# Spreading the rows of max plus log-sum over SBUF: from eight partitions instead of from DRAM

## The chip, the cores and the metric

The kernel runs on one core of one Trainium2 chip. A core has TensorE (PE; PEld is its weight load), VectorE (DVE), ScalarE (ACT), GpSimd (POOL), SyncE (SP, which issues every DMA of this kernel) and 16 DMA engines. The metric is the device time of one execution in microseconds; lower is better.

## The reference

For 8 batches, 8 heads, 576 tokens and a head width of 64, a linear attention is followed by a gated mixing layer:

```python
q_s = exp(q - max(q, -1)); q_s = q_s / (sum(q_s, -1) + 1e-09)      # over a head's 64 channels
k_s = exp(k - max(k, 2));  k_s = k_s / (sum(k_s, 2) + 1e-09)       # over the 576 tokens
kv  = einsum('bhsd,bhse->bhde', k_s, v)
x   = einsum('bhsd,bhde->bhse', q_s, kv)        # heads laid side by side: (B, S, 512)
gate = sigmoid(causal 5-tap convolution of x along the tokens, a tap per channel)
out  = (gate * (x @ w_val)) @ w_out             # all float32
```

## The kernel before

Everything works by batch and, inside a batch, by four blocks of 128 channels (two heads each); a block holds all 576 tokens in the free dimension. Each engine runs its instructions in the order in which a hand-written list, `ORDER`, names the steps (`name batch block engine`); nothing is reordered afterwards. An engine that waits holds up all that stands behind it on that engine. Matmuls take float32 split into a high and a low part (`x_high`, `x_low` and so on), so every product is three matmuls.

The softmax of q runs along the channels of a head, but the attention matmul (`attend`) wants channels on partitions. For batches 4 to 7 the kernel therefore computes, with tokens on partitions, the max (`q_max`), the exponentials and their sum (`q_total`), takes the logarithm (`q_log`, on ACT), and brings max plus log of the sum to the channel layout, where `l_sub` subtracts it from q as loaded by channel (`load_qc`) and `c_exp` takes the exponential: exp(q - max - log sum) is the softmax. The steps that bring it there are the ones changed:

- `l_turn` (L403): one addition of `qm` and `qs` into the tile `lse` (128 tokens by head and chunk of 128 tokens), and four 32 by 64 transposes on DVE into `lt`, a buffer of the rotating two-buffer tag `far`. Then a row of `lt` holds 128 tokens of one head.
- `l_row` (L411): two DMAs write those 40 rows into a DRAM tile `lrow`, a head's five chunks one behind the other.
- `l_spread` (L418): DMAs read a head's row from DRAM once for each of the 64 partitions of the head and so fill `lb` (128 partitions, four blocks, 576 tokens; 1.18 MB). The even heads go to partitions 0 to 63 and the odd heads to 64 to 127. The last 64 tokens of an odd batch sit in the row of the even batch before it, so an even batch takes two DMAs and an odd batch four.
- `l_sub` (L428): four subtractions `qc - lb` per batch, one per channel block, on POOL or DVE.

The tag `far` is also used by the convolution: `far` (ACT, L574) writes one scaled tap into a buffer of it, and `near` (POOL, L579) adds that to the gate. With two buffers, the second `far` after an `l_turn` gets the buffer in which `lt` was.

All DMAs go out on SP in list order, on one hardware queue, and the program has eight DMA semaphores that the DMAs take in turn: one DMA is not issued before the one eight places ahead of it has landed.

Of the kernel before, what the change touches and what calls it, by code (L numbers as in the profile page):

```python
# [7 lines left out]
F32 = mybir.dt.float32  # L8
# [8 lines left out]
B, H, S, D = 8, 8, 576, 64  # L17
C = H * D
P = 128
NB = C // P  # L20
MAIN = 4 * P
# [5 lines left out]
PITCH = 5 * P  # L27
# [123 lines left out]
def gated_linear_attention(ctx: ExitStack, tc: tile.TileContext, q, k, v, qt, kt, vt, qc, kc, km, w_val, w_out, ident_in, out):  # L151
    nc = tc.nc

    const = ctx.enter_context(tc.tile_pool(name="const", bufs=1))
# [3 lines left out]
    rowpool = ctx.enter_context(tc.tile_pool(name="rowpool", bufs=1, space=bass.MemoryType.DRAM))  # L158
# [5 lines left out]
    def block(tag, name, bufs, dtype=F32, n=S):  # L164
        return work.tile([P, S], dtype, tag=tag, name=name, bufs=bufs)[:, :n]
# [21 lines left out]
    T = {}  # L187
# [7 lines left out]
    def q_parts(b):  # L195
        return 5 if b % 2 == 0 else 4
# [204 lines left out]
    def l_turn(b):  # L401

        n = q_parts(b)  # L403
        lse, turned = lses[b % 2], T.setdefault(("lt", b), block("far", f"lt_{b}", 2)[:32, :2 * P].rearrange("p (k r) -> p k r", k=2))
        by_chunk = [t[:, :n * H].rearrange("p (c h) -> p c h", h=H) for t in (T["qm", b], T["qs", b])]
        nc.vector.tensor_add(lse[:, :5 * H].rearrange("p (h c) -> p c h", c=5)[:, :n], *by_chunk)
        for g in range(4):
            gs = slice(32 * g, 32 * g + 32)
            nc.vector.transpose(turned[:, :, gs], lse[gs].rearrange("p (k r) -> p k r", k=2))

    def l_row(b):  # L411

        t = T["lrow", b] = rowpool.tile([H * PITCH], F32, tag=f"lrow{b}", name=f"lrow{b}")
        rows_of = t.rearrange("(r s) -> r s", s=P)
        nc.sync.dma_start(out=rows_of[:32], in_=T["lt", b][:, 0])
        nc.sync.dma_start(out=rows_of[32:], in_=T["lt", b][:5 * H - 32, 1])

    def l_spread(b):  # L418
        t = big.tile([P, 5, C], F32, tag="q", name=f"lb{b}").rearrange("p c j -> p (c j)")[:, :NB * S]
        t = T["lb", b] = t.rearrange("p (n s) -> p n s", n=NB)  # L420
        pieces = [(b, 0, slice(0, S))] if b % 2 == 0 else [(b, 0, slice(0, MAIN)), (b - 1, S, slice(MAIN, S))]
        for j in range(2):
            for row, at, cs in pieces:
                n = cs.stop - cs.start
                one = T["lrow", row].rearrange("(p j s) -> j p s", j=2, s=PITCH)[j:j + 1, :, at:at + n]
                nc.sync.dma_start(out=t[D * j:D * j + D, :, cs], in_=one.broadcast_to([D, NB, n]))

    def l_sub(b, p, e="p"):  # L428
        t = T["qc", b, p]
# [214 lines left out]
        [const.tile([P, NB, C], F32R, tag=f"{w}_{x}", name=f"{w}_{x}") for x in ("hi", "lo")]  # L644
        for w in ("w_val", "w_out")
    ]
    lses = [const.tile([P, 64], F32, tag=f"lse{i}", name=f"lse{i}") for i in range(2)]
    kvd = [const.tile([P, NB, P], F32, tag=f"kvd{i}", name=f"kvd{i}") for i in range(2)]
    ktz = [const.tile([P, C], F32, tag=f"ktz{i}", name=f"ktz{i}") for i in range(2)]
    nc.scalar.preload_act_table(AF.Exp)  # L650
    for t in kvd + ktz + lses:
        nc.gpsimd.memset(t, 0.0)

    with tc.manual_schedule():
# [51 lines left out]
```

## Time and profile before

| | us |
|---|---|
| median of the runs (308.83 to 309.14) | 308.99 |
| profiled execution | 311.52 |
| its span | 309.6 |
| PE busy | 275.5 (89%) |
| DVE busy | 270.4 (87%) |
| ACT busy | 223.6 (72%) |
| POOL busy | 220.4 (71%) |
| mean rate of the DMAs | 196 GB/s |

The span is the time from the first to the last instruction of the profiled execution; 1.9 us of its time lie around it. A row of a timeline gives the start, the duration, the engine, the source line, and, in brackets, how long the engine was idle ahead of it and what ended that. In a row of windows, the last three numbers are the granted TensorE clock, the busy share of the 16 DMA engines and the rate that they moved.

### The profile page before, as it was taken

Reading aid. Unit: us, or ns where it says so; the run is one execution under the profiler, and the core shown is the slowest. Engines: PE = TensorE matmul, PEld = TensorE weight load, DVE = VectorE, ACT = ScalarE, POOL = GpSimd, SP = SyncE. Lnnn points to the kernel's source line nnn. Section 1 sums busy time; section 2 is a strip of 40 time slices with the busy share of each in tenths; the row PEclk is TensorE's granted clock in tenths of the full one; section 3 lists DMA queues with packets and bytes.
Section 4 is the critical chain, followed back from the end, with each engine's and each line's share of the span. In section 5 each row is a group of like instructions: output and inputs, shape, how many; then the busy total and the mean of one; then the engine's idle time right before and its main releaser. Section 6 shows DMA issues by size and latency. Waiting matters only on the chain.

```text
span 309.6 us, 6401 instructions
## 1 busy us (share of the span) xinstructions
PE 275.5 (89%) x2464; PEld 266.5 (86%) x2464; DVE 270.4 (87%) x371; ACT 223.6 (72%) x356; POOL 220.4 (71%) x196
## 2 busy tenths in 40 slices
PE   0176899999999999799977999997989999999995
PEld 0066699999999999799966999897989999999994
DVE  3899999999999997999899999999998898777721
ACT  2898999949997798779966697894966694426100
POOL 4678777799987998894989439596469856925600
PEclk9997999999999999889999799999999999999999
DMA  7999622688829999537867786895159330011012
GB/s 213 407 412 372 229 92 70 282 249 310 293 26 376 286 389 296 236 98 177 274 257 173 152 266 216 290 228 217 16 181 238 100 116 2 8 71 76 2 45 108
DMA packets 23278, 60.77 MB, mean 196 GB/s; under 512 B 4272, under 2 KB 4816, under 8 KB 20560
## 3 DMA queue, kind: packets, MB, share of 16 engines
q1 hardware_dynamic: 23248, 60.37, 60.0%
q8 instruction: 19, 0.31, 0.4%
q14 instruction: 11, 0.09, 0.1%
HBM read 50.83 MB, written 9.53 MB: 195 GB/s over the span
## 4 chain that ended last, share of the span: by engine, by line
PE 62%; DVE 18%; DMA 9%; ACT 4%; issue 4%; POOL 1%; SPq 1%; DVEq 0%; ACTq 0%
PE out L595 26%; PE val L595 24%; PE kv L468 5%; PE x L548 5%; DVE gate L572 3%; DMA k<-in_k 3%; DMA kc<-in_k_channels 3%; DMA q<-in_q 3%; PE qTps L500 2%; DVE g L613 2%; DMA out<-o 2%; DVE gl L621 1%; DVE q L375 1%; DVE x L567 1%; DVE qm L370 1%
## 5 line engine op out<-in xcount | busy, mean ns | idle before, releaser
L595 PE MATMUL val<-x,w_val_hi 128*128 128x288 f32 x512 | 88.4, 294 | 0.0
L572 DVE SCALAR_TENSOR_TENSOR gate<-x,cw,gate 128x574 f32<-128x574 f32 (+3 forms) x103 | 82.4, 808 | 2.4 <-ACT far L577 0.7
L595 PEld LDWEIGHTS val<-x,w_val_hi 128*128 128x128 f32 x512 | 74.8, 188 | 0.0
L595 PE MATMUL out<-gh,w_out_lo 128*128 128x288 f32 x256 | 57.4, 304 | 2.6 <-DVE g L613 1.9
L595 PE MATMUL val<-x,w_val_lo 128*128 128x288 f32 x256 | 55.4, 297 | 3.0 <-DVE o L177 1.8
L595 PE MATMUL out<-gh,w_out_hi 128*128 128x288 f32 x256 | 56.1, 299 | 0.0
L595 PEld LDWEIGHTS out<-gh,w_out_lo 128*128 128x128 f32 x256 | 41.8, 191 | 4.4 <-issue 2.1
L581 POOL TENSOR_TENSOR gate<-gate,far 128x572 f32<-128x572 f32 (+3 forms) x25 | 34.2, 1371 | 15.9 <-ACT far L577 10.7
L595 PEld LDWEIGHTS val<-x,w_val_lo 128*128 128x128 f32 x256 | 40.8, 188 | 3.8 <-ACT gate L584 1.9
L595 PE MATMUL out<-gl,w_out_hi 128*128 128x288 f32 x256 | 41.1, 302 | 1.9 <-DVE gl L621 1.9
L595 PEld LDWEIGHTS out<-gh,w_out_hi 128*128 128x128 f32 x256 | 42.2, 192 | 0.0
L595 PEld LDWEIGHTS out<-gl,w_out_hi 128*128 128x128 f32 x256 | 37.4, 196 | 2.3 <-DVE gl L621 2.3
L621 POOL TENSOR_TENSOR gl<-g,gh 128x576 fp32r<-128x576 f32 x19 | 27.6, 1459 | 12.4 <-ACT gh L175 7.0
L175 ACT COPY o<-out 128x576 f32<-128x576 f32 (+1 forms) x24 | 15.1, 629 | 26.8 <-PE out L595 16.6
L375 POOL TENSOR_TENSOR q<-q,qm 128x512 f32<-128x512 f32 x28 | 31.3, 1130 | 3.8 <-PE val L595 2.3
L310 POOL TENSOR_TENSOR k<-k,kmax 128x512 f32<-128x512 f32 x21 | 28.3, 1359 | 2.7 <-DMA kmax<-krow 2.6
L613 DVE TENSOR_TENSOR g<-val,gate 128x576 f32<-128x576 f32 x32 | 23.8, 749 | 7.0 <-PE val L595 6.8
L584 ACT ACTIVATE gate<-gate 128x576 f32<-128x576 f32 x32 | 21.5, 682 | 10.7 <-DVE gate L572 6.9
L577 ACT ACTIVATE far<-x,cw 128x572 f32<-128x572 f32 (+3 forms) x25 | 18.6, 743 | 13.4 <-DVE gate L563 4.8
L430 POOL TENSOR_TENSOR qc<-qc,lb 128x576 f32<-128x576 f32 x13 | 18.9, 1464 | 10.1 <-DMA qc<-in_q_channels 9.1
L370 DVE TENSOR_REDUCE qm<-q 128x8 f32<-128x512 f32 (+3 forms) x12 | 20.8, 1743 | 4.9 <-DMA q<-in_q 3.2
L567 DVE TENSOR_TENSOR x<-x,x 128x576 fp32r<-128x576 f32 x32 | 23.9, 748 | 0.1
(108 smaller groups left out, 556.5 us busy)
## 6 DMA issues: line engine op xcount, KB each, us to landing
out<-o SPq DMA_DIRECT2D x31, 288.0 KB, 3.9
v<-in_v SPq DMA_DIRECT2D x8, 1040.0 KB, 7.5
q<-in_q SPq DMA_DIRECT2D x7, 1024.0 KB, 7.6
km<-in_k_strided SPq DMA_DIRECT2D x24, 288.0 KB, 5.7
k<-in_k SPq DMA_DIRECT2D x6, 1024.0 KB, 7.8
qc<-in_q_channels SPq DMA_DIRECT2D x16, 288.0 KB, 4.9
kc<-in_k_channels SPq DMA_DIRECT2D x8, 288.0 KB, 8.1
lb<-lrow SPq DMA_DIRECT2D x4, 576.0 KB, 7.5
```

The costliest lines, as they stand in the source:

```text
L310: engine(e).tensor_sub(kk[r, cs], kk[r, cs], mx[r, cs])
L370: nc.vector.tensor_reduce(out=T["qm", b][:, cs], in_=qq, axis=AX.X, op=ALU.max, negate=b < 2)
L375: engine(e).tensor_tensor(qq, qq, m, op=ALU.add if b < 2 else ALU.subtract)
L430: engine(e).tensor_sub(t, t, T["lb", b][:, p])
L567: nc.vector.tensor_sub(xl, T["x", b, p], T["xh", b, p].bitcast(F32))
L572: nc.vector.scalar_tensor_tensor(out=a, in0=x, scalar=w, in1=a, op0=ALU.mult, op1=ALU.add)
L577: nc.scalar.activation(T["far", b, p, j], T["x", b, p][:, :S - n], AF.Copy, scale=cw[:, p, j:j + 1])
L581: nc.gpsimd.tensor_add(a, a, T["far", b, p, j])
L584: nc.scalar.activation(T["gate", b, p], T["gate", b, p], AF.Sigmoid)
L595: nc.tensor.matmul(ps[:, cs], a[:, kb, ms], z[:, cs], start=(i == 0), stop=(i == len(parts) - 1))
L613: nc.vector.tensor_mul(T["g", b, m], T["val", b, m], T["gate", b, m])
L621: engine(e).tensor_sub(T["gl", b, m], T["g", b, m], T["gh", b, m].bitcast(F32))
```

## The change

`l_turn` now transposes into partitions 32 to 63 of the whole `far` buffer. Its rows are ordered by head and chunk with four chunks a head; the fifth chunk, which only even batches have, is added by an instruction of its own and lies in eight further rows. There is one `lse` tile where there were two.

`l_row` no longer writes to DRAM. One DMA gathers, inside the same buffer, the four pieces of each head into one row on partitions 0 to 7, a partition for each head. In an even batch a second DMA brings the first half of the fifth chunk behind it, and a third saves the second half, the tail of the odd batch, in a small tile `ltail`; an odd batch fetches its tail from `ltail`.

`l_spread` issues eight DMAs, one for each head, in the order of the heads. Each reads one partition's row of 576 numbers 64 times and writes it to the 64 partitions of the head: 144 KB each.

```diff
     def l_turn(b):
 
         n = q_parts(b)
-        lse, turned = lses[b % 2], T.setdefault(("lt", b), block("far", f"lt_{b}", 2)[:32, :2 * P].rearrange("p (k r) -> p k r", k=2))
-        by_chunk = [t[:, :n * H].rearrange("p (c h) -> p c h", h=H) for t in (T["qm", b], T["qs", b])]
-        nc.vector.tensor_add(lse[:, :5 * H].rearrange("p (h c) -> p c h", c=5)[:, :n], *by_chunk)
+        t = T["lt", b] = block("far", f"lt_{b}", 2)
+        qm, qs = (x[:, :4 * H].rearrange("p (c h) -> p c h", h=H) for x in (T["qm", b], T["qs", b]))
+        nc.vector.tensor_add(lse[:, :32].rearrange("p (h c) -> p c h", c=4), qm, qs)
+        if n == 5:
+            nc.vector.tensor_add(lse[:, 32:32 + H], T["qm", b][:, 4 * H:], T["qs", b][:, 4 * H:])
+        k = n - 3
         for g in range(4):
             gs = slice(32 * g, 32 * g + 32)
-            nc.vector.transpose(turned[:, :, gs], lse[gs].rearrange("p (k r) -> p k r", k=2))
+            out = t[32:64, :k * P].rearrange("p (k r) -> p k r", k=k)[:, :, gs]
+            nc.vector.transpose(out, lse[gs, :32 * k].rearrange("p (k r) -> p k r", k=k))
 
     def l_row(b):
 
-        t = T["lrow", b] = rowpool.tile([H * PITCH], F32, tag=f"lrow{b}", name=f"lrow{b}")
-        rows_of = t.rearrange("(r s) -> r s", s=P)
-        nc.sync.dma_start(out=rows_of[:32], in_=T["lt", b][:, 0])
-        nc.sync.dma_start(out=rows_of[32:], in_=T["lt", b][:5 * H - 32, 1])
+        t = T["lt", b]
+        nc.sync.dma_start(out=t[:H, :MAIN], in_=t[32:64, :P])
+        if b % 2 == 0:
+            nc.sync.dma_start(out=t[:H, MAIN:], in_=t[32:32 + H, P:P + 64])
+            nc.sync.dma_start(out=ltail, in_=t[32:32 + H, P + 64:2 * P])
+        else:
+            nc.sync.dma_start(out=t[:H, MAIN:], in_=ltail)
 
     def l_spread(b):
         t = big.tile([P, 5, C], F32, tag="q", name=f"lb{b}").rearrange("p c j -> p (c j)")[:, :NB * S]
         t = T["lb", b] = t.rearrange("p (n s) -> p n s", n=NB)
-        pieces = [(b, 0, slice(0, S))] if b % 2 == 0 else [(b, 0, slice(0, MAIN)), (b - 1, S, slice(MAIN, S))]
-        for j in range(2):
-            for row, at, cs in pieces:
-                n = cs.stop - cs.start
-                one = T["lrow", row].rearrange("(p j s) -> j p s", j=2, s=PITCH)[j:j + 1, :, at:at + n]
-                nc.sync.dma_start(out=t[D * j:D * j + D, :, cs], in_=one.broadcast_to([D, NB, n]))
+        for h in range(H):
+            one = T["lt", b][h:h + 1].unsqueeze(1).broadcast_to([1, D, S])
+            nc.sync.dma_start(out=t[D * (h % 2):D * (h % 2) + D, h // 2], in_=one)
...
-    lses = [const.tile([P, 64], F32, tag=f"lse{i}", name=f"lse{i}") for i in range(2)]
+    lse = const.tile([P, 64], F32, tag="lse", name="lse")
+    ltail = const.tile([H, 64], F32, tag="ltail", name="ltail")
...
-    for t in kvd + ktz + lses:
+    for t in kvd + ktz + [lse]:
```

On SP, around the spread of batch 4 (`lt_4` is the transposed tile, `lb4` the spread one, `kmax_5` the spread max of k, `out_0` the result), there stood before:

```order
L300 DMA krow5_1755<-kpk_5_1493 128x4
L415 DMA lrow4_1765<-lt_4_1757 32x128
L416 DMA lrow4_1765<-lt_4_1757 8x128
L220 DMA qc_4_0_1811<-in_q_channels 128x576
L638 DMA out_0<-o_2_1_1780 128x576
L426 DMA lb4_1823<-lrow4_1765 64x4x576 x2
L220 DMA qc_4_2_1896<-in_q_channels 128x576
L213 DMA q6_1898<-in_q 128x2048
```

And now:

```order
L300 DMA krow5_1754<-kpk_5_1492 128x4
L418 DMA lt_4_1756<-lt_4_1756 8x4x128
L420 DMA lt_4_1756<-lt_4_1756 8x64
L421 DMA ltail_79<-lt_4_1756 8x64
L220 DMA qc_4_0_1811<-in_q_channels 128x576
L642 DMA out_0<-o_2_1_1780 128x576
L430 DMA lb4_1823<-lt_4_1756 64x1x576 x8
L220 DMA qc_4_2_1902<-in_q_channels 128x576
L213 DMA q6_1904<-in_q 128x2048
```

No step changed its place; two DMAs have become three for the rows, and two have become eight for the spread, all ahead of the same loads. The four heads' worth of one DMA before are now four DMAs.

On DVE, the additions and transposes of batches 4 and 5 before:

```order
L406 TENSOR_TENSOR lse0_78<-qm_4_1376,qs_4_1683 128x5x8
L409 STREAM_TRANSPOSE lt_4_1757<-lse0_78 32x2x32 x4
...
L406 TENSOR_TENSOR lse1_79<-qm_5_1619,qs_5_1863 128x4x8
L409 STREAM_TRANSPOSE lt_5_1946<-lse1_79 32x2x32 x4
```

And now:

```order
L406 TENSOR_TENSOR lse_78<-qm_4_1375,qs_4_1682 128x4x8
L408 TENSOR_TENSOR lse_78<-qm_4_1375,qs_4_1682 128x8
L413 STREAM_TRANSPOSE lt_4_1756<-lse_78 32x2x32 x4
...
L406 TENSOR_TENSOR lse_78<-qm_5_1618,qs_5_1869 128x4x8
L413 STREAM_TRANSPOSE lt_5_1952<-lse_78 32x32 x4
```

An even batch has one addition more, and an odd batch transposes half as much. The orders on PE and ACT are the same as before, and so is POOL's but for one memset less. Because the spread now reads from the `far` buffer, the ACT instruction that writes that buffer next (`far 3 1 0` for batch 4) now waits for all eight spread DMAs, where before the buffer was free once the two row DMAs had landed.

## The prediction

> **What bounds the kernel now.** I read the page first, then the chain of waits, then the changed tile `lb` by itself, and last the windows and timelines around its four transfers.
>
> ```profile
> span 309.6 us, 6401 instructions
> PE 62%; DVE 18%; DMA 9%; ACT 4%; issue 4%; POOL 1%; SPq 1%; DVEq 0%; ACTq 0%
> GB/s 213 407 412 372 229 92 70 282 249 310 293 26 376 286 389 296 236 98 177 274 257 173 152 266 216 290 228 217 16 181 238 100 116 2 8 71 76 2 45 108
> ```
>
> The chain of waits runs mostly over PE, then DVE. The DMA engines reach 412 GB/s at most, so each of the 16 moves at most 412 / 16 = 25.8 GB/s. From the chain, in order of time, two pieces say which engine carries it behind the changed steps:
>
> ```profile
> 221.23 2.21 DVE qs L394
> ...
> 230.32 3.44 PE val L595 x24
> ...
> 252.25 2.48 PE kv L468 x80
> ```
>
> From 199 to 230 us the chain is DVE, from there to the end PE, and it passes through no spread. The tile `lb` by itself (instructions, then its waits, then the time from issue to landing):
>
> ```profile
> L430 POOL TENSOR_TENSOR qc<-qc,lb x13: 1404/1425/1947, 148.1 to 249.1; 128x576 f32<-128x576 f32 x13
> L426 SPq DMA_DIRECT2D lb<-lrow x12: 586/609/1162, 138.0 to 235.3; - x12
> ...
>   DMA lb<-lrow: 0.9, 1
> ...
> DMA to landing us min/median/max: 6.3/7.4/8.5
> ```
>
> Only one subtraction waits for `lb`, 0.9 us. So there is almost nothing to win by a faster spread, and a slower one is late soon. The SyncE timeline gives the issue of the four spreads, batches 4 to 7:
>
> ```profile
> 138.04 1.35 SPq L426 DMA_DIRECT2D lb<-lrow  x2
> 163.69 2.56 SPq L426 DMA_DIRECT2D lb<-lrow  x4
> 199.99 1.25 SPq L426 DMA_DIRECT2D lb<-lrow  x2
> 232.73 3.14 SPq L426 DMA_DIRECT2D lb<-lrow  x4
> ```
>
> How fast do they move? Windows, first of a stretch with 128-partition loads, then three with the spreads of batches 6 and 7 (last three numbers: clock, DMA share, GB/s):
>
> ```profile
> 196.00:200.00 4.00, 3.38 (x26) 3.14 (x24) 4.00 (x6) 3.47 (x6) 1.42 (x2) 1.00 0.99 350
> ...
> 204.00:206.00 2.00, 2.00 (x17) 2.00 (x16) 2.00 (x3) 1.71 (x4) 2.00 (x2) 1.00 1.06 222
> ...
> 236.00:238.00 2.00, 2.00 (x18) 2.00 (x17) 1.93 (x4) 1.20 (x1) 1.92 (x3) 1.00 1.05 212
> 238.00:240.00 2.00, 2.00 (x17) 2.00 (x17) 1.97 (x4) 0.00 (x0) 1.92 (x2) 1.00 1.07 211
> ```
>
> This is the row on which the forecast rests. The engines are equally busy, but a transfer that has 64 partitions at its SBUF end moves 211 to 222 GB/s, half of the 412 of the page. The rate follows the number of partitions that a DMA reaches, not the engines. The changed spread has 64 partitions at one end and **one** at the other.
>
> **The rows (`l_turn`, `l_row`).** An even batch has one addition more, an odd batch half the transposing.
>
> ```profile
> L409 DVE STREAM_TRANSPOSE lt<-lse x16: 232/233/238, 134.2 to 229.2; 32x64 f32<-32x64 f32 x16
> L406 DVE TENSOR_TENSOR lse<-qm,qs x4: 293/615/1245, 133.8 to 227.2; 128x40 f32<-128x40 f32 x2, 128x32 f32<-128x32 f32 x2
> L415 SPq DMA_DIRECT2D lrow<-lt x4: 325/359/380, 135.2 to 229.4; - x4
> SPq L426 <- DMA lrow<-lt: 3.5, 1, 3.5
> ```
>
> Two additions at 0.3 us and up to eight times 0.12 us saved cancel within 1 us. The gather costs SP a third DMA in even batches, 0.4 us by the row of L415. What could be won is the wait of SP for the rows in DRAM, 3.5 us once (the last row above), but the spread that it holds back is not waited for there. I take the steps at nothing; if the gather were as slow as DRAM, that is what the kernel has now.
>
> **The spread.** The bytes stay: 128 partitions x 4 x 576 x 4 = 1.18 MB, 147,456 B for a head. Call X the time from the issue of the first of the eight DMAs to the landing of the last. Bounds for the rate:
> - From above, the source sets no limit: 215 GB/s as in the windows, X about 1.18 MB / 215 + landing = 7 to 8.5 us, as now.
> - From below, strict proportion to the partitions: 412 / 128 = 3.2 GB/s, 46 us for one head.
> - Between them: one partition hangs on one of sixteen ways, and a way carries a sixteenth of the peak, 25.8 GB/s. Then a head takes 147,456 / 25.8e3 = 5.7 us.
>
> I take the middle one. Half the partitions gave half the rate, so the ways are limited, and the best that the trace shows one engine to carry is 25.8. The eight heads go one after the other, since all DMAs are on one queue and all engines have the first head's rows ahead of the next one's: 8 x 5.7 = 45.8, and with 1.5 us to land (144 KB stores land in 1.8 us, of which 0.4 is their bytes) X = 47.3 us.
>
> ```profile
> out<-o SPq DMA_DIRECT2D x2, 144.0 KB, 1.8
> ```
>
> [...]
>
> **What the late spread costs, batch by batch.** Rows of before, the first instructions that need the spread and what hangs on them:
>
> ```profile
> 144.54 0.78 ACT L577 ACTIVATE far<-x,cw 128x572 f32<-128x572 f32 x1
> 146.63 0.23 ACT L399 ACTIVATE qs<-qs 128x32 f32<-128x32 f32 x1
> ...
> 147.25 0.93 DVE L406 TENSOR_TENSOR lse<-qm,qs 128x32 f32<-128x32 f32 x1
> 155.29 2.82 DVE L370 TENSOR_REDUCE qm<-q 128x40 f32<-128x2560 f32 x1 [1.67 <-DMA q<-in_q_tail]
> ...
> 175.02 1.43 POOL L430 TENSOR_TENSOR qc<-qc,lb 128x576 f32<-128x576 f32 x1 [3.92 <-DMA qc<-in_q_channels]
> 176.40 1.04 POOL L375 TENSOR_TENSOR q<-q,qm 128x512 f32<-128x512 f32 x1
> 181.69 2.34 ACT L379 ACTIVATE q<-q 128x2560 f32<-128x2560 f32 x1
> 184.06 2.82 DVE L394 TENSOR_REDUCE qs<-q 128x40 f32<-128x2560 f32 x1
> ...
> 209.39 2.81 POOL L430 TENSOR_TENSOR qc<-qc,lb 128x576 f32<-128x576 f32 x2
> 212.15 1.49 POOL L375 TENSOR_TENSOR q<-q,qm 128x512 f32<-128x512 f32 x1
> 219.01 1.92 ACT L379 ACTIVATE q<-q 128x2048 f32<-128x2048 f32 x1
> ...
> 243.22 1.43 POOL L430 TENSOR_TENSOR qc<-qc,lb 128x576 f32<-128x576 f32 x1 [0.85 <-DMA lb<-lrow]
> 244.60 1.41 POOL L581 TENSOR_TENSOR gate<-gate,far 128x572 f32<-128x572 f32 x1
> 245.97 1.76 POOL L310 TENSOR_TENSOR k<-k,kmax 128x512 f32<-128x512 f32 x1
> ```
>
> - Batch 4: the `far` buffer now stays taken until the last head has landed. `far 3 1 0` on ACT (144.54, 6.5 us behind the issue) waits for it, and behind it stand the logarithm of batch 5 (146.63) and so DVE's addition (147.25). The 1.67 us for which DVE waits at 155.29 go into that. Delay X - 6.5 - 1.7 = X - 8.2.
> - Batch 5: `l_sub 5 3` on POOL needs heads 6 and 7 and the `qc` loads queued behind them, 2 x 295 KB / 350 GB/s = 1.7 us more. Then 1.4 (`l_sub`) and 1.0 (`q_sub`), and ACT can start the exponential of q, which DVE takes up at once (184.06): X + 4.1 against 181.69 - 163.69 = 18.0. Delay X - 13.9.
> - Batch 6: the two `l_sub` on POOL need `qc` loads that now land behind all heads, 0.8 us; then 2.8 and 1.5, and ACT's exponential, at 219.01 or 19.0 behind the issue, feeds DVE's sum at 221.23, in the chain. Delay X + 5.1 - 19.0 = X - 13.9.
> - Batch 7: POOL's `l_sub 7 3`, then `near` and `k_sub`, 1.4 + 1.4 + 1.8, then ACT's exponential of k, 1.9; TensorE's `kv 7` in the chain at 252.25, 19.5 behind the issue, needs it. Delay X + 6.5 - 19.5 = X - 13.0.
>
> TensorE has work queued for a few microseconds at each of these places, but DVE or PE, in the chain, stands behind each of the four. Nor can the loads behind the spread (q and k of the next batches) pass it: they land during the same stall. The sum is 4X - 49.0 = 4 x 47.3 - 49.0 = 140 us on the profiled execution's 311.5, so 452; the median of the runs is 2.5 us lower, so **449 us**. After such gaps the clock is halved for a while:
>
> ```profile
> 172.00:174.00 2.00, 2.00 (x10) 2.00 (x10) 1.96 (x4) 0.27 (x1) 0.00 (x0) 0.50 0.59 190
> ```
>
> That may cost some 2 us a gap; it is left to the range.
>
> **The rivals.**
> - *The source sets no limit*, because repeated reads of one row are served as easily as those of DRAM, or are read once. This is the other side: no slower. For it: `lb<-lrow`, too, reads each row 64 times and fills its 64 partitions at half the peak. Against it: the halving itself. Price: X is 8, every delay in the list is nil or negative, and the eight issues (8 x 0.6 = 4.9 us on SP) lie beside the transfer. What can be won is the 0.9 us at 243 us, what can be lost is 1.5 us at `far 3 1 0`. Time 308 to 313, from X under some 10 us on.
> [...]
> - *Strict proportion* or worse than a sixteenth: one partition gives less than a way does. Half a way would be 4 x 93 - 49 = 323 us more, time over 600. Nothing in the trace asks for it.
>
> **How the numbers follow.** One way, one after the other: 0.58; no limit: 0.22 (of that 0.04 faster, 0.17 the same, 0.01 slower by over 2%); two ways: 0.14; worse: 0.06. The forecast's own range is 432 (5.3 us a head, and 3 us of slack found in each batch) to 462 (2 us a gap for the clock, and some for the loads behind). To leave out no more than 2 in 10 the range goes from 310, which takes in most of the case without a limit, to 462. It is wide because the cost of reading one partition 64 times stands in no row. Within 2% is what a measurement here can't tell from no change; slower by more than that 0.58 + 0.14 + 0.06 + 0.01 = 0.79, the same 0.17, faster 0.04.
>
> **What would show it.** In the changed profile, the eight `lb<-lt` DMAs should land 5 to 6 us apart, and the windows from their issue should show the DMA rate near 26 GB/s with the engines' share near 1. ACT should wait at `far` (now L581) for `lb` or `lt` some 40 us in batch 4, POOL at `l_sub` (now L434) for `lb` over 30 us in batches 5 to 7, and PE should have four gaps. `lb` issues that land in 8 us or less, with no new wait at L434 above 2 us, would prove it wrong; landing 2.9 us apart on the mean would be the two ways.

## The result: 445 us, 1.44 times the time before

The changed kernel takes 444.88 us (443.67 to 446.08) against 308.99 us; the ratio is 1.440, with a 95% interval from 1.423 to 1.457. The forecast was 449 us. Its profiled execution took 443.67 us with a span of 441.9, so 132.3 us more than the span before.

The page of the changed kernel: the span, the rate of the DMAs in 40 slices of 11 us, and the chain of waits.

```profile
span 441.9 us, 6438 instructions
...
GB/s 270 411 306 222 93 217 326 212 248 298 360 217 92 27 37 29 198 181 49 28 32 44 261 255 120 29 33 41 191 105 127 27 34 40 116 9 55 53 2 107
...
SPq 34%; PE 27%; DMA 17%; DVE 9%; POOL 6%; issue 4%; ACT 3%; DVEq 0%; POOLq 0%; ACTq 0%
```

Before, 62% of the chain was PE and 1% SP's queue. Now 34% is SP's queue, PE is 27%. Four times the rate falls to 27 to 49 GB/s for three or four slices: those are the four spreads. Their issues in SyncE's timeline, batches 4 to 7:

```profile
138.47 31.10 SPq L430 DMA_DIRECT2D lb<-lt  x8
...
200.18 30.51 SPq L430 DMA_DIRECT2D lb<-lt  x8
...
267.30 30.55 SPq L430 DMA_DIRECT2D lb<-lt  x8
...
334.32 30.75 SPq L430 DMA_DIRECT2D lb<-lt  x8
```

The issues before were at 138.04, 163.69, 199.99 and 232.73. So the delay grows by 36.1 us behind batch 4, 30.8 behind batch 5, 34.3 behind batch 6, and from 101.6 to the 132.3 at the end, 30.7 behind batch 7. The four stalls are the whole difference. Inside the first of them, from the chain, the single issues:

```profile
138.47 0.57 SPq L430
139.09 0.58 SPq L430
139.73 1.14 SPq L430
140.91 7.92 SPq L430
148.87 5.45 SPq L430
154.37 5.44 SPq L430
159.85 4.23 SPq L430
164.12 5.44 SPq L430
```

From the fourth on, SP is held at every issue: 7.92 us at the fourth, 4.23 at the seventh and 5.44 or 5.45 at the others, instead of 0.6. 5.44 us is the pace of a head: 147,456 B in 5.44 us are 27.1 GB/s. The windows inside the stall and behind it say the same (clock, DMA share, GB/s at the end):

```profile
150.00:160.00 10.00, 0.00 (x0) 0.00 (x0) 0.00 (x0) 0.00 (x0) 0.00 (x0) 0.52 0.88 29
...
182.00:186.00 4.00, 2.92 (x54) 2.92 (x56) 3.68 (x8) 3.94 (x6) 2.89 (x3) 0.50 0.92 321
```

The 16 engines count as 88% busy and move 29 GB/s, while every compute engine stands. Who waits first, from the timelines of ACT, POOL and DVE:

```profile
181.38 0.74 ACT L581 ACTIVATE far<-x,cw 128x572 f32<-128x572 f32 x1 [37.35 <-DMA qc<-in_q_channels]
...
244.66 0.74 ACT L581 ACTIVATE far<-x,cw 128x572 f32<-128x572 f32 x1 [30.20 <-DMA qc<-in_q_channels]
...
246.26 1.40 POOL L434 TENSOR_TENSOR qc<-qc,lb 128x576 f32<-128x576 f32 x1 [39.30 <-DMA qc<-in_q_channels]
...
311.34 2.75 POOL L434 TENSOR_TENSOR qc<-qc,lb 128x576 f32<-128x576 f32 x2 [33.38 <-DMA qc<-in_q_channels]
...
312.90 0.76 DVE L177 COPY o<-out 128x576 f32<-128x576 f32 x1 [30.73 <-DMA out<-o]
...
377.96 1.40 POOL L434 TENSOR_TENSOR qc<-qc,lb 128x576 f32<-128x576 f32 x1 [35.81 <-DMA lb<-lt]
...
378.74 0.76 DVE L177 COPY o<-out 128x576 f32<-128x576 f32 x1 [32.77 <-DMA out<-o]
```

In batch 4 it is `far 3 1 0` on ACT, whose buffer the spread still reads (it waits for the eight spread DMAs; the profile names a transfer that came last with them). In batches 5, 6 and 7 it is the first `l_sub` on POOL. Beside it stand waiters that the forecast did not have. In batch 5 `far` on ACT waits 30.20 us and goes on 1.6 us before POOL does. In 6 and 7 it is DVE's copy of a result, whose buffer is free only when an earlier store has left, and that store is queued behind the spread. From first issue to the end of the wait, X is 181.38 - 138.47 = 42.9 us in batch 4 and 377.96 - 334.32 = 43.6 us in batch 7.

### The profile page after: what moved, and what is told of

It reads as the page before. It is cut to its first block, busy times and chain, and to the rows that moved or that the text cites. A ratio compares the mean times of both kernels' runs of the same rounds, so it can differ in the third digit from the quotient of the medians.

```text
span 441.9 us, 6438 instructions
## 1 busy us (share of the span) xinstructions
PE 281.5 (64%) x2464; PEld 270.9 (61%) x2464; DVE 273.5 (62%) x373; ACT 223.8 (51%) x356; POOL 221.3 (50%) x195
## 4 chain that ended last, share of the span: by engine, by line
SPq 34%; PE 27%; DMA 17%; DVE 9%; POOL 6%; issue 4%; ACT 3%; DVEq 0%; POOLq 0%; ACTq 0%
SPq L430 27%; PE val L599 12%; PE out L599 9%; DMA out<-o 7%; SPq L220 5%; DMA qc<-in_q_channels 5%; PE kv L472 2%; DMA v<-in_v 2%; DMA kc<-in_k_channels 2%; PE x L552 2%; PE qTps L504 2%; DMA q<-in_q 2%; DVE qm L370 1%; POOL k L310 1%; POOL gl L625 1%
## 5 line engine op out<-in xcount | busy, mean ns | idle before, releaser
L599 PE MATMUL val<-x,w_val_hi 128*128 128x288 f32 x512 | 91.9, 302 | 28.3 <-DVE x L571 28.3
L576 DVE SCALAR_TENSOR_TENSOR gate<-x,cw,gate 128x574 f32<-128x574 f32 (+3 forms) x103 | 82.3, 807 | 39.1 <-ACT far L581 37.4
L599 PE MATMUL val<-x,w_val_lo 128*128 128x288 f32 x256 | 58.4, 311 | 64.7 <-DVE o L177 62.0
L599 PEld LDWEIGHTS val<-x,w_val_hi 128*128 128x128 f32 x512 | 78.2, 195 | 28.5 <-DVE x L571 28.5
L599 PEld LDWEIGHTS val<-x,w_val_lo 128*128 128x128 f32 x256 | 43.2, 199 | 66.1 <-ACT qc L438 31.4
L177 DVE COPY o<-out 128x576 f32<-128x576 f32 (+1 forms) x9 | 6.5, 722 | 74.0 <-DMA out<-o 63.5
L472 PE MATMUL kv<-v,k 128*64 128x65 f32 x512 | 21.4, 235 | 38.5 <-DVE gate L576 36.7
L472 PEld LDWEIGHTS kv<-v,k 128*64 128x64 f32 x512 | 19.5, 149 | 40.3 <-DVE gate L576 36.9
L599 PE MATMUL out<-gl,w_out_hi 128*128 128x288 f32 x256 | 39.7, 295 | 1.5 <-DVE gl L625 1.5
L599 PEld LDWEIGHTS out<-gl,w_out_hi 128*128 128x128 f32 x256 | 35.7, 188 | 1.9 <-DVE gl L625 1.9
L625 POOL TENSOR_TENSOR gl<-g,gh 128x576 fp32r<-128x576 f32 x19 | 27.6, 1460 | 9.9 <-ACT gh L175 6.9
L438 ACT ACTIVATE qc<-qc 128x576 f32<-128x576 f32 x16 | 10.6, 680 | 37.2 <-POOL qc L434 37.2
```

The lines of the kernel that those rows point to most:

```text
L472: nc.tensor.matmul(acc[h * D:(h + 1) * D, p, :], T["k", b][:, c, cs] if c < 4 else ktz[b % 2][:, cs], T["v", b][:, c, hd] if c < 4 else T[ ...
L576: nc.vector.scalar_tensor_tensor(out=a, in0=x, scalar=w, in1=a, op0=ALU.mult, op1=ALU.add)
L599: nc.tensor.matmul(ps[:, cs], a[:, kb, ms], z[:, cs], start=(i == 0), stop=(i == len(parts) - 1))
L625: engine(e).tensor_sub(T["gl", b, m], T["g", b, m], T["gh", b, m].bitcast(F32))
```

## Experiments

The theory: a source partition's way into the DMA sets the pace, and all that is queued behind the spread waits with it. The rivals: the eight DMAs themselves; SBUF as a source; the single partition, or the receiving side, rather than a way that partitions share; and the waits for `lb` and for the `far` buffer rather than the queue. Where no ratio is given, the time is that of a single execution.

### The rows in DRAM again, eight DMAs kept

```diff
...
-        pieces = [(b, 0, slice(0, S))] if b % 2 == 0 else ...
...
+        row = T["lrow", b].rearrange("(h s) -> h s", s=PITCH)
+        for h in range(H):
+            one = row[h:h + 1, :S].unsqueeze(1).broadcast_to([1, D, S])
+            nc.sync.dma_start(out=t[D * (h % 2):D * (h % 2) + D, h // 2], in_=one)
```

> The kernel before, with its rows in DRAM, but with the spread issued as eight DMAs of 144 KB, one for each head, as in the changed kernel; an odd batch fetches its 64-token tail by one small DMA from DRAM to DRAM. My theory (one SBUF partition as the source of 64 reads sets the pace, 5.4 us a head): the source is DRAM again, so a spread lands in some 8 us at about 215 GB/s and the time is 308 to 314 us. The rival (eight small DMAs, their issue on SP and the eight semaphores are what costs): SP stands at each of them for about 5 us as in the changed kernel, and the time stays above 400 us.

Measured: 310.11 us, ratio 1.002 (0.998 to 1.006). The tile `lb` of this kernel:

```profile
L429 SPq DMA_DIRECT2D lb<-lrow x32: 445/594/606, 137.1 to 239.8; - x32
...
DMA to landing us min/median/max: 3.0/3.6/5.2
```

The same eight transfers, with the same 64 reads of one row, take 0.6 us to issue and land in 3.6 us when the row is in DRAM. So neither the number of DMAs nor the repeated reading as such shows in the time. The source is left.

### SBUF as the source, but 64 partitions of it

```diff
-            one = T["lt", b][h:h + 1].unsqueeze(1).broadcast_to([1, D, S])
+            one = W[0][0].bitcast(F32).rearrange("p n c -> p (n c)")[D * (h % 2):D * (h % 2) + D, :S]
```

> The changed kernel, but each of the eight DMAs of a spread reads 64 different SBUF partitions of a constant (the high part of w_val) instead of one partition 64 times; bytes, targets and number of DMAs stay. The spread rows are then not the max plus log-sum, so the output is another. My theory: 64 source partitions feed it about as fast as it is written, a spread lands in 8 us, 306 to 314 us. The rival (SBUF as a source is slow, or SBUF to SBUF at all): 440 us or near it.

Measured: 309.37 us, ratio 1.003 (0.998 to 1.008). The tile `lb`:

```profile
L430 SPq DMA_DIRECT2D lb<-w_val_hi x32: 461/598/1571, 137.3 to 236.6; - x32
...
DMA to landing us min/median/max: 2.6/3.7/5.1
```

SBUF to SBUF is as fast as DRAM to SBUF here. This kernel also has all the rest of the change: the additions, the halved transposes, the gather inside SBUF and the eight DMAs. Together they cost and bring nothing that can be measured. The `far` buffer is also free earlier here, since the spread reads another tile; the slow spread that nobody waits for, below, reads one partition at a time of that same tile and takes 440 us, so it is not the tile that helps. The 132 us hang on one thing, that each DMA reads one partition.

### Heads of the two groups in turn

```diff
-        for h in range(H):
+        for h in (0, 4, 1, 5, 2, 6, 3, 7):
...
```

> The changed kernel with the heads of a spread in the order 0, 4, 1, 5, 2, 6, 3, 7, so that neighbours in the queue come from the two groups of four source partitions. In the changed kernel one boundary of the seven (head 3 to head 4) has its issue some 1.2 us sooner than the pace of 5.45 us; the others do not. My theory (the four partitions share one way, and only the next row of an engine's queue is fetched ahead): all seven boundaries overlap a little, X falls from 43.5 by 6 x 1.2 = 7 us, the time by four times that, to about 417 us. If each engine kept two ways busy: X halves, 360 us. If the limit belonged to the single partition or to the receiving side: 444 us, as it is.

Measured: 382.17 us, which none of the three cases had. A window of the first stall, then POOL's wait in batch 7 and the issue of that spread:

```profile
148.00:154.00 6.00, 0.00 (x0) 0.00 (x0) 0.00 (x0) 0.00 (x0) 0.00 (x0) 0.50 0.78 49
```

```profile
316.20 1.40 POOL L434 TENSOR_TENSOR qc<-qc,lb 128x576 f32<-128x576 f32 x1 [18.40 <-DMA lb<-lt]
```

```profile
289.82 19.22 SPq L430 DMA_DIRECT2D lb<-lt  x8
```

The order alone takes 62 us off. 49 GB/s is nearly twice 27, and X is 26.4 us. With heads 0 and 4 as neighbours in the queue 49 GB/s are moved, with heads 0 and 1 as neighbours 27.1, although each head has a partition of its own. So the limit is neither the partition nor the receiving side, but something that partitions 0 to 3 share and that 4 to 7 do not share with them; a way is a name for it here. My step "only the next row is fetched ahead", which gave 417 us, was wrong. That engines that are through with one head's rows go on to the next head's, so that both ways are busy most of the time, would fit 49 against 27, but is a guess: no view shows the engines one by one.

### Pieces of 16 partitions, two groups in turn

```diff
-        for h in range(H):
+        for i in range(4):
+            for q in range(4):
+                for h in (i, i + 4):        # 16 partitions from D * (h % 2) + 16 * q
...
```

> The changed kernel with each head's DMA cut into four of 16 partitions (36 KB, one row for each of the 16 DMA engines), and the pieces of heads h and h + 4 alternating in the queue. Every next row of an engine then comes from the other group of four partitions. My theory: with one row fetched ahead, both ways work at once, X is about 22 to 24 us (32 issues of 0.55 us are 18 us), and by 4X - 49 the time is 350 to 360 us. The rival (strictly one row at a time on an engine, or a limit that is not in the source partitions): X stays at 43 us or more, and so 440 us.

Measured: 365.63 us, X 24.8 us (274.42 to 299.20). A window of its first stall:

```profile
154.00:160.00 6.00, 0.00 (x0) 0.00 (x0) 0.00 (x0) 0.00 (x0) 0.00 (x0) 0.74 0.94 52
```

That is near twice 27.1. The first case came out, 6 us later than its range. But the 32 issues take 21.8 us, 0.68 us for each 36 KB, and the issue alone would so give 54 GB/s. The run shows 52 GB/s from the two groups, and not whether they or the issue set the limit.

### Partitions 32 apart

```diff
...
-        for h in range(H):
-            one = T["lt", b][h:h + 1]...
+        for h in (0, 4, 1, 5, 2, 6, 3, 7):
+            r = h if h < 4 else 28 + h
+            one = T["lt", b][r:r + 1]...
```

> The kernel with alternating heads (0, 4, 1, 5, 2, 6, 3, 7), but with the rows of heads 4 to 7 on partitions 32 to 35 instead of 4 to 7 (and the transposed rows on 64 to 95). [...] If a way belongs to neighbouring partitions alone: as with 4 to 7, near 382 us.

Measured: 453.84 us, 10 us above the changed kernel's profiled execution and far from 382. A window of its first stall:

```profile
156.00:166.00 10.00, 0.00 (x0) 0.00 (x0) 0.00 (x0) 0.00 (x0) 0.00 (x0) 0.50 0.90 28
```

The order that gave 49 GB/s with heads 4 to 7 on partitions 4 to 7 gives 28 with them on 32 to 35; X is 46.2 us. The order and the target partitions are the same in both, so the receiving side is not what differs. So partitions 0 to 3 and 32 to 35 share a way (28 GB/s together), and 4 to 7 have another (49 together with 0 to 3). These three groups are all that was run: which other partitions share a way, and how many ways there are, is not shown.

### Partitions four apart

The rows of the heads on partitions 0, 4, ... 28, heads in order:

```diff
-        nc.sync.dma_start(out=t[:H, :MAIN], in_=t[32:64, :P])
+        nc.sync.dma_start(out=t[0:32:4, :MAIN], in_=t[32:64, :P])
...
-            one = T["lt", b][h:h + 1]...
+            one = T["lt", b][4 * h:4 * h + 1]...
```

> The changed kernel with the eight rows on partitions 0, 4, 8, ... 28 instead of 0 to 7, heads in order, eight DMAs of 144 KB as in the changed kernel. If the limit is a way shared by four neighbouring partitions, and engines that are through with one head go on to the next (as the run with alternating heads showed: 49 to 52 GB/s from two ways), then eight ways feed the spread: it is limited by its receiving side, 215 GB/s, and by eight issues, X is 8 to 12 us, and the time is 308 to 318 us. If a single partition limits, whatever its neighbours: little changes, 380 to 444 us.

Measured: 372.19 us, ratio 1.206 (1.193 to 1.219): neither case. POOL's wait in batch 7, and the issue of that spread:

```profile
305.20 1.40 POOL L434 TENSOR_TENSOR qc<-qc,lb 128x576 f32<-128x576 f32 x1 [16.93 <-DMA lb<-lt]
```

```profile
279.89 17.65 SPq L430 DMA_DIRECT2D lb<-lt  x8
```

X is 25.3 us, 1.18 MB in that time are 47 GB/s, 1.7 times 27.1, from eight partitions. That each of the eight has a way of its own is an assumption, carried on from partitions 0 to 3 and 4 to 7; the other groups were not set against each other. But the same partitions move more below, so they are not what sets 47: a second limit stands behind the first. Two more kernels cut the heads finer, all first pieces ahead of all second ones, so that neighbours in the queue always read from partitions at least four apart:

```diff
+        for q in range(2):                  # or range(4)
+            for h in range(H):              # 32 partitions a piece, or 16
...
```

> The rows on eight ways (partitions 0, 4, ... 28), and each head's DMA cut into two of 32 partitions (two rows for an engine), all first halves ahead of all second halves, 16 DMAs a spread. With whole heads the eight ways gave X = 25 us, no more than two ways' worth. If what limits is how many rows an engine has under way (about four, so that they reach into the next head and no further), two rows a piece let three or four ways work at once: X 13 to 18 us, time 330 to 345 us. If only two neighbouring DMAs can overlap, whatever their size: X stays near 25 us, time near 370 us.

Measured: 338.94 us. POOL's wait and the issue in batch 7:

```profile
272.44 1.40 POOL L436 TENSOR_TENSOR qc<-qc,lb 128x576 f32<-128x576 f32 x1 [10.84 <-DMA lb<-lt]
```

```profile
253.36 14.44 SPq L432 DMA_DIRECT2D lb<-lt  x16
```

The time is in the range of the first case, and X, 19.1 us, is 1 us above its own. Over the whole spread that is about 62 GB/s; a window in the middle of the first one moves 87 GB/s, 3.2 times 27.1:

```profile
148.00:152.00 4.00, 3.45 (x24) 3.21 (x24) 0.48 (x1) 2.54 (x3) 0.00 (x0) 1.00 0.99 87
```

> The rows on eight ways and pieces of 16 partitions (one row for an engine), in the order of the heads, 32 DMAs a spread. The issue alone takes 32 x 0.6 = 19 us, so X is 21 to 23 us at best if four or more ways work at once, and the time 340 to 350 us. If only two neighbouring DMAs overlap: X 25 us or more, 365 us or more, as with two alternating ways.

Measured: 362.57 us, X 23.5 us (271.51 to 295.03), between the two cases: 13 us above the range of the first and 2 us below the second. The issues take 0.65 us each, 21 us in all. The landings of `lb` tell which it is:

```profile
DMA to landing us min/median/max: 2.8/2.9/4.0
```

Each piece lands 2.9 us after its issue (the median); pieces of the same size from partitions 0 to 7 took 4.2 us. So hardly any stands behind another here: the issue is the limit, and the run can't tell how many ways would work at once.

What follows: from the same eight partitions the spread as a whole moves 47 GB/s in DMAs of 64 rows and 62 in DMAs of 32. Neither rate is steady: in windows of 6 us the first is 43 and 67 (146 to 158 us), in windows of 4 us the second 70, 85 and 87 (140 to 152 us), so 47 and 62 are means. The rise would agree with a fixed, small number of rows that an engine has under way. If a DMA's rows are shared out evenly over the 16 engines, an engine has four rows of a head or two of a half, and the author's estimate from these rates is four to six under way: more than the four rows of one head, up to three half heads of two. No view shows it, and the issue takes over before one row a piece can say more. None of these kernels beats the one before, and there is little to win: before, one subtraction waited 0.9 us for `lb`.

### The slow spread, and nobody waits for it

```diff
-            one = T["lt", b][h:h + 1].unsqueeze(1).broadcast_to([1, D, S])
+            one = W[0][0].bitcast(F32).rearrange("p n c -> p (n c)")[h:h + 1, :S].unsqueeze(1).broadcast_to([1, D, S])
...
-        engine(e).tensor_sub(t, t, T["lb", b][:, p])
+        engine(e).tensor_sub(t, t, W[0][0].bitcast(F32).rearrange("p n c -> p (n c)")[:, :S])
```

> The changed kernel, with the same slow spread on the queue (eight DMAs that read one partition each 64 times, of the constant w_val high part), but nobody waits for it: l_sub subtracts the constant itself, and the far buffer is free once the rows are gathered. The softmax of q in batches 4 to 7 is so left out of the computation. My theory says that the loads behind it on the one queue can't pass, so their lateness alone costs nearly as much: q and qc loads land some 43 us after the spread's issue, and the time stays above 400 us. The rival: the waits for lb and for the far buffer are the cost, and without them the time is near 310 us.

Measured: 439.68 us, 4 us below the changed kernel's profiled execution. The first waits of each batch, from the timelines of DVE and POOL:

```profile
181.81 0.76 DVE L434 TENSOR_TENSOR qc<-qc,w_val_hi 128x576 f32<-128x576 f32 x1 [32.17 <-DMA qc<-in_q_channels]
...
308.17 0.76 DVE L177 COPY o<-out 128x576 f32<-128x576 f32 x1 [29.46 <-DMA out<-o]
...
374.02 0.76 DVE L177 COPY o<-out 128x576 f32<-128x576 f32 x1 [30.59 <-DMA out<-o]
```

```profile
240.94 1.40 POOL L434 TENSOR_TENSOR qc<-qc,w_val_hi 128x576 f32<-128x576 f32 x1 [37.32 <-DMA qc<-in_q_channels]
```

With `lb` unread and the `far` buffer free, loads of q by channel and stores of results that stand behind the spread make the same stalls. One wait for the spread is left here: at 175 us SP holds a load of q for 5.9 us until `lb` has landed. So the waits for `lb` and `far` may cost a little more than the 4 us, but to remove them alone would win almost nothing. Whether loads on another queue would pass the spread was not run.

### Time against X

X of batch 7 (from the first issue to the end of POOL's wait) and the span above the 309.6 us of before, for the kernels that read one partition a DMA and whose `l_sub` reads `lb`:

| kernel | X | span added | 4X - 42 |
|---|---|---|---|
| four apart, halves | 19.1 | 27.6 | 34 |
| four apart, pieces of 16 | 23.5 | 51.2 | 52 |
| two groups, pieces of 16 | 24.8 | 54.3 | 57 |
| four apart, whole heads | 25.3 | 59.8 | 59 |
| two groups, heads in turn | 26.4 | 70.8 | 64 |
| the change | 43.6 | 132.3 | 132 |
| 32 apart | 46.2 | 142.5 | 143 |

The 42 is taken from the row of the change. The slope of four, one stall for each spread, holds over the whole range to within some 7 us: a straight line through the seven rows has a slope of 4.1, though from 19 to 26 us alone it is steeper.

## Why the prediction was right

- **The rows at nothing.** Right: the kernel that keeps all of the change but the single source partition is at 1.003.
- **The rate from one partition.** Right in kind: the middle bound, a way that one source partition hangs on. The 25.8 GB/s, a sixteenth of the highest slice, was 5% low against the measured 27.1. X was put at 47.3 us and is 42.9 to 43.6. That there are sixteen ways, one for each engine, was the author's estimate; no run shows their number.
- **One head after the other.** Right for this order, with one exception that supports it: the seventh issue takes 4.23 us instead of 5.44 (4.70 in batch 5, 4.20 in batch 7). SP runs some three DMAs ahead of the transfers, since it is held from the fourth issue on, so this is about where heads 3 and 4, from the two groups, meet. After four heads of 5.44 us, at 160 us, one window of 2 us moves 70 GB/s, where those from 144 to 160 us move 25 to 34:

```profile
160.00:162.00 2.00, 0.00 (x0) 0.00 (x0) 0.00 (x0) 0.00 (x0) 0.00 (x0) 0.50 0.91 70
```

The reason given, that all engines have the first head's rows ahead, does not hold by itself: in another order the same DMAs move 49 GB/s.
- **The four stalls.** Forecast 39.1, 33.4, 33.4 and 34.3 us; measured 36.1, 30.8, 34.3 and 30.7. The waiters named (`far` on ACT, then `l_sub` on POOL three times) are in the trace, with 37.4, 39.3, 33.4 and 35.8 us. The profile puts only the last of them down to `lb`, the others to `qc` loads on the same queue.
- **The constant of the sum.** This term was mis-sized: the slack came to 42 us instead of 49. With the measured X the formula would have given 125 instead of 132. With X at 42.9 us in batch 4 and taken as 43.6 in the others, its terms are 34.7, 29.7, 29.7 and 30.6, so most of the 7 us, 4.6, lies behind batch 6. There the chain does not run over `l_sub` and the exponential, as forecast, but over DVE's copy, which waits for a store queued behind the spread; the stores were not in the sum. The chain from that copy to the next product `g`, before and after:

```profile
214.92 0.67 DVE o L177
...
219.40 0.74 DVE g L613
```

```profile
312.90 0.77 DVE o L177
313.80 5.15 PE val L599 x24
319.08 0.76 DVE g L617
```

The copy comes 30.7 us later against the spread's issue than before. From it to `g` it takes 6.2 us instead of 4.5, as the 24 matmuls take 5.15 us: from 313 to 317 us the granted clock is 0.50, as in the gaps. Then SP needs 5.0 us instead of 3.3 from its first row DMA (329.28, before 229.45) to the spread of batch 7. That makes 34.2 of the 34.3 us. How the other 2.6 us divide over batches 4, 5 and 7 is open.
- **What made the end come out.** X too long by 4 us, times four, is 15 us too much; the slack overrated by 7 us is 7 too little. The errors partly cancel, and 449 lies 4 us from 444.9; that it lies so near is in part luck.
- **The lower end of the range.** Its 432 does not follow from its terms: 5.3 us a head gives 436, and 3 us of slack in each of four batches would take it to 424.
- **The rivals.** That the source sets no limit fell: the spread is as fast as before from DRAM (1.002) and from 64 partitions (1.003), not from one. Two ways at once, given 0.14, is not what this kernel does; another order of the same DMAs moves 49 GB/s and takes 382 us. Strict proportion to the partitions fell, at 27.1 GB/s against 3.2.

## What to carry to other kernels

A row that 64 partitions need was read from DRAM at 211 to 222 GB/s, as fast as 64 partitions were written here, but from one SBUF partition at 27 GB/s, fifteen times below the peak of 412. To spread 144 KB so takes 5.4 us, and rows on partitions 0 to 3, read one behind the other, moved no faster together. Ask of a DMA not only how many partitions it writes but how many it reads, and what it delays: on the one queue of this kernel the slow spread made the loads and stores behind it late by 29 to 37 us a batch even when nobody waited for its data (439.68 us). The busy share of the DMA engines, 0.88 in the stall, does not show this; only the rate beside it, 29 GB/s, does.

## What the hardware showed that was not expected

- The issuing instruction itself blocks: with some three DMAs of 144 KB on the way, SP stands 5.44 us at most further issues, 31 us a spread, where the same DMAs from DRAM are issued in 0.6 us each.
- Eight source partitions four apart give whole heads only 47 GB/s over the spread; half heads, 62.
- The engines' busy share is 0.88 to 0.90 at 28 to 29 GB/s.
